# Giving the operations that empty a PSUM bank an earlier place in the scheduler's order

## The chip, the cores and the metric

The kernel runs on one NeuronCore of a Trainium2 chip. The metric is the device time of one execution in microseconds (us). Five engines matter: TensorE (PE in the profile) does matrix products into PSUM, which has eight banks of 128 partitions by 2 KB; VectorE (DVE) and ScalarE (ACT) work on PSUM and SBUF; GpSimd (POOL) and SyncE (SP) mainly issue DMA transfers here. Each engine runs its own list of instructions in the order in which the program was laid out, and waits on semaphores for the others.

## The reference

Eight sequences of 3008 positions with 256 channels go through a filter in the frequency domain, and every position of the result then goes through a two-layer network with a squared relu.

```python
X  = rfft(x, axis=1)                       # x: 8 x 3008 x 256
Yr = Xr @ w_r - Xi @ w_i + b_r
Yi = Xr @ w_i + Xi @ w_r + b_i
Y  = sign(Y) * max(abs(Y) - 0.01, 0)       # on Yr and Yi each
y  = irfft(Y, n=3008, axis=1).reshape(24064, 256)
out = (s * max(y @ w_in, 0)**2 + b) @ w_out    # d_ff 2048, back to 256
```

The inputs and the result are float32; the kernel's products take float16 operands and sum in float32.

## The kernel before, in words

**The transforms.** 3008 is 94 x 32, so both transforms are done as two smaller ones, as matrix products. For a batch there are four kinds of unit, each of which fills one PSUM bank and ends with an operation that empties it:
- `s1_units`: the first step (products `psf<-x,A_t`), emptied to `u` by `evac`, which goes out to DRAM as `ud` and comes back turned as `us`.
- `s23_units`: `fwd_unit` (`psf<-F_t,us`), emptied to `xf` by `evac`, and then the sum of two parts of `xf` on DVE (L672); `sum_unit` (`psf<-W_t,xf`), emptied to `s` by ACT (L686); `mix_unit` (`psf<-W_g,xf`), emptied by a DVE add into a buffer called `ring` (L699). `shrink` is the soft threshold on `ring` in three DVE operations (L714, L715, L716), after which SP moves the quarters of `ring` by DMA (L725). `inv_unit` (`psf<-ring,T_t`) is emptied to `v` by `evac`, and `v` goes through DRAM too.
- `s4_units`: the last step (`psf<-C_t,vs`), emptied to `yt` by `evac`. `yt` holds what the network takes as its tokens.

`evac` puts its copy on ACT (L187) or on DVE (L189), by two running estimates of how far each engine's work reaches (`load`, `work`, `act_first`).

**The network.** The token phase, which begins after the first batch's transforms, goes over tiles of up to 512 tokens. A tile has 16 slots (MC = 16 blocks of the hidden width). In slot `mc`, `first_mm` computes one block of `y @ w_in` into half of a double bank (`psh`); every second slot ACT applies the relu to `rt` (L871), and the square goes to `gt` on ACT (L881) or DVE (L884). The product with `w_out` of a tile runs one tile later, in slots beside the next tile's `first_mm`. It comes in two forms:
- `second_mms`: plain products into a `psa` bank, two halves to a bank, and one DVE operation that empties it to `ost` (L945).
- `seven_mms`, for some tiles: a block scheme with seven products in place of eight. It needs sums of blocks of `gt`, made in `s_op`: numbers 1, 2 and 3 on DVE (L980), number 4 as an accumulating DMA issued by POOL (L973). The products share banks in the groups (0, 1), (2), (3, 4) and (5, 6). `leave(group)` combines them: in group 0 an add into `zz` (L1012), an add into `ost` (L1012) and then `zz` plus a constant (L1030); in groups 1 to 3 more adds by L1012. The output goes to DRAM by SP's queue.

**Sharing the banks.** In the token phase the pools hold two double banks (`psh`), two single banks for the network's second product (`psa`) and two for the transforms (`psf`). A matmul that opens a bank anew waits until the operation that empties the bank's previous tile has ended.

**Sharing the time.** `plan` puts the units of the next batches' transforms into the slots of the current tiles, so that the program's text interleaves `first_mm`, the second product and transform units. All matmuls are issued by one helper and so carry one line, L175; the tiles' names tell them apart.

**What sets the order.** The framework numbers operations as the program issues them. When it lays out each engine's list, it goes by this number as priority among the operations that it deems ready by a model of its own. Inside `tc.high_priority(offset=200)` an operation gets a number 200 lower, so that it counts as if it had been issued 200 places earlier. An operation's place in one engine's list can also change what is deemed ready on another.

Of the kernel before, what the change touches and what calls it, by code (L numbers as in the profile page):

```python
# [1 line left out]

# [1 line left out]

# [7 lines left out]
ALU = mybir.AluOpType  # L12
AF = mybir.ActivationFunctionType

P = 128
# [81 lines left out]
def kernel(  # L97
# [79 lines left out]
    def work(engine, us):  # L177
        load[engine] = max(load[engine], pe["now"]) + us

    def act_first(ready, ta, td):  # L180
        return max(load["act"], ready) + ta <= max(load["dve"], ready) + td + lean[0]

    def evac(dst, src, cols):
        ta, td = over["act"] + cols / 1200.0, over["dve"] + cols / 960.0
        if act_first(pe["now"], ta, td):
            work("act", ta)
            return None, nc.scalar.copy(out=dst, in_=src)  # L187
        work("dve", td)
        return nc.vector.tensor_copy(out=dst, in_=src), None  # L189

    pools = {}

# [456 lines left out]
    def s23_units(b):  # L649

        vd = dpool.tile([NPAIR, P, D], F16, name="vd", tag="vd")
        if not ring:
            ring.append(bigpool.tile([P, 12, 2, D], F16, name="ring", tag="corr"))
        xf = {}
        zt = {}
        hold = {}

        def fwd_unit(i):

            bank = one_bank()  # L660
            ps = bank.rearrange("p (r c j k) -> p r c j k", r=2, c=DC, j=2)
            t = us[(b, i // 3)]
            for j in range(2):
                q = (2 * i + j) % 6
                for dc in range(DC):
                    matmul(
                        ps[:, :, dc, j, :], t[:, q, dc * P : (dc + 1) * P],
                        F_t[:, 2 * i + j, :], start=True, stop=True,
                    )
            xt = xfpool.tile([P, 3, DC, P], F16, name="xf", tag="xf")  # L670
            evac(xt[:, 1:3].rearrange("p r c k -> p (r c k)"), bank, 512)
            nc.vector.tensor_tensor(out=xt[:, 0], in0=xt[:, 1], in1=xt[:, 2], op=ALU.add)  # L672
            work("dve", 0.34)
            xf[i] = xt

        def sum_unit(h):

            ps = one_bank().rearrange("p (i e) -> p i e", i=2)
            for i in range(2):
                for dc in range(DC):  # L680
                    matmul(
                        ps[:, i, :], xf[2 * h + i][:, 0, dc], W_t[:, dc, 0],
                        start=(dc == 0), stop=(dc == DC - 1),
                    )
            s = mpool.tile([P, 2, D], F32, name="s", tag="m")
            nc.scalar.copy(out=s, in_=ps)  # L686
            work("act", 0.49)
            hold[h] = s

        def mix_unit(i):  # L690
            ps = one_bank().rearrange("p (r e) -> p r e", r=2)
            xt = xf.pop(i)
            for r in range(2):
                for dc in range(DC):
                    matmul(
                        ps[:, r, :], xt[:, 2 - r, dc], W_g[:, dc, r],
                        start=(dc == 0), stop=(dc == DC - 1),
                    )
            nc.vector.tensor_tensor(  # L699
                out=ring[0][:, i % 4], in0=ps,  # L700
                in1=hold[i // 2][:, i % 2].unsqueeze(1).to_broadcast([P, 2, D]), op=ALU.add,
            )
            work("dve", 0.67)
            if b == 1:
                shrink(i, 1)
            elif i % 2:
                shrink(i - 1, 2)

        def shrink(i, n):

            m0 = 4 + (i % 2 if n == 1 else 0)
            t, m = ring[0][:, i % 4 : i % 4 + n], ring[0][:, m0 : m0 + n]
            lo, hi = (v.unsqueeze(1).to_broadcast([P, n, 2, D]) for v in (low, high))
            nc.vector.tensor_tensor(out=m, in0=t, in1=lo, op=ALU.max)  # L714
            nc.vector.tensor_tensor(out=m, in0=m, in1=hi, op=ALU.min)  # L715
            nc.vector.tensor_tensor(out=t, in0=t, in1=m, op=ALU.subtract)  # L716
            work("dve", 0.21 + 0.8 * n)
            for k in range(i, i + n):
                z = ring[0][:, 6 + k % 6]
                for j in range(2):  # L720
                    for r in range(2):
                        o = z[64 * r : 64 * r + 64, j]
                        a = t[64 * j : 64 * j + 64, k - i, r]
                        if k < H - 2:
                            nc.sync.dma_start(out=o, in_=a)  # L725
                        else:
                            nc.vector.tensor_copy(out=o, in_=a)
                            work("dve", 0.13)
                zt[k] = z

        def inv_unit(i):
            ps = one_bank().rearrange("p (j e) -> p j e", j=2)
            z = zt.pop(i)
            for j in range(2):
                matmul(
                    ps[:, j, :], T_t[:, 2 * i + j, :], z[:, j, :], start=True, stop=True
                )
            if i % 2 == 0:
                hold["v"] = vpool.tile([P, 4, D], F16, name="v", tag="v")
            v = hold["v"]  # L740
            h = 2 * (i % 2)
            evac(v[:, h : h + 2, :], ps, 512)
            if i % 2 == 1:
                nc.sync.dma_start(
                    out=vd[2 * i - 2 : 2 * i + 2].rearrange("q p e -> p q e"), in_=v
                )
            if i == H - 1:
                hold["vv"] = vd.rearrange("q (k n) e -> (q k) (n e)", n=N2)
                take_half(0)
                if b == 1:  # L750
                    take_half(1)

        def take_half(h):
            t = vspool.tile([96, HW, D], F16, name="vs", tag="vs")
            nc.sync.dma_start(
                out=t.rearrange("k n e -> k (n e)"),
                in_=hold["vv"][:, h * HW * D : (h + 1) * HW * D],
            )
            vs[(b, h)] = t

        units = []

        def put(f, i, n):
            if 0 <= i < n:
                units.append(lambda: f(i))

        for h in range(H // 2 + 3):
            for i in range(2):
                put(fwd_unit, 2 * h + i, H)
                put(mix_unit, 2 * h - 2 + i, H)  # L770
                put(inv_unit, 2 * h - 6 + i, H)
            put(sum_unit, h, H // 2)
            if h == H // 2:
                units += [lambda: None] * 2
        return units, lambda: take_half(1)
# [75 lines left out]
    def first_mm(ti, mc):  # L851
# [16 lines left out]
        if mc % 2 == 0:  # L868
            return
        rt = rpool.tile([P, 2, 512], F32, name="rt", tag="rt")  # L870
        nc.scalar.activation(out=rt[:, :, 0:w], in_=ps[:, :, 0:w], func=AF.Relu)  # L871
        q, g = divmod(mc // 2, 4)
        if g == 0:
            gts[(ti, q)] = gpool.tile([P, 2, 2, 4, 2 * P], F16, name="gt", tag="gt")
# [47 lines left out]
    def second_mms(ti):  # L922
# [6 lines left out]
        def mm(sub, mc):  # L929

            alone = ti == len(tiles) - 1 and sub >= 2
            h = 0 if alone else sub % 2
            if h == 0 and mc == 0:
                hold["ps"] = sum_bank(ti).rearrange("p (h e) -> p h e", h=2)
            ps = hold["ps"]
            matmul(
                ps[0:size, h, :],
                lhs_of(ti, mc, sub),
                w_out_t[:, mc, :],
                start=(mc == 0), stop=(mc == MC - 1),  # L940
            )
            if mc == MC - 1 and (alone or h == 1 or sub == nsub - 1):
                k = h + 1
                ost = opool.tile([P, 2, D], F32, name="ost", tag="ost")
                nc.vector.scalar_tensor_tensor(  # L945
                    out=ost[0:size, 0:k], in0=ps[0:size, 0:k], scalar=s_bc[0:size],
                    in1=bias_bc[0:size].unsqueeze(1).to_broadcast([size, k, D]), op0=ALU.mult, op1=ALU.add,
                )
                work("dve", 0.13 + 0.27 * k)
                for i in range(k):  # L950
                    store(tl, sub - k + 1 + i, ost[:, i, :])
# [31 lines left out]
    def seven_mms(ti):  # L983
# [25 lines left out]
            )  # L1009

        def add(out, of, other):
            nc.vector.scalar_tensor_tensor(  # L1012
                out=out, in0=of, scalar=s_bc[0:size], in1=other, op0=ALU.mult, op1=ALU.add
            )
            work("dve", 0.4)

        def wide(t):
# [2 lines left out]
        def leave(group):  # L1020
# [6 lines left out]
            if group == 0:  # L1027
                add(z[:, 0], hold[0], wide(bias_bc))
                add(top[:, :, 0:P], hold[1], z[:, 0])
                nc.vector.tensor_tensor(out=z[:, 1], in0=z[:, 0], in1=wide(b_21), op=ALU.add)  # L1030
                work("dve", 0.34)
            elif group == 1:
                add(z[:, 0], hold[2], z[:, 0])
# [144 lines left out]
```

## Time and profile before

The times of three runs are 840.66, 837.92 and 838.69 us; the median is 838.69. The profile was taken of one execution.

| | |
|---|---|
| profiled execution: span, first to last instruction | 837.9 us |
| median of the runs, less this span | 0.8 us |
| PE busy (matmuls) | 822.6 us, 98%, 7662 matmuls |
| ACT busy | 723.0 us, 86%, 962 instructions |
| DVE busy | 706.9 us, 84%, 1104 instructions |
| POOL busy | 86.2 us, 10%, 114 instructions |
| granted clock of TensorE, mean | 0.996 |
| DMA moved | 107.17 MB, mean 128 GB/s |

The page gives each engine's busy time, the span in 40 slices, the DMA queues, the chain of work that ended last, groups of equal instructions with the idle time before them, and the DMA issues. A group is written as out<-in by the program's names, such as `psa<-T_s,s`. The trace behind it also answers questions of its own: what an engine waited for and how long (the list of waits), what ran in a stretch of time (the timeline, where a bracket at the end of a row is idle time of the engine before it and what ended it), and who waits for one line's instructions.

### The profile page before, as it was taken

The page shows a single profiled execution, that of the slowest core. Times are in us where ns is not written, and L with a number is a line of the kernel's source. Part 1 is how long each engine was busy: PE and PEld are TensorE (multiplying, and loading weights), DVE is VectorE, ACT ScalarE, POOL GpSimd, SP SyncE. Part 2 cuts the span into 40 slices and gives each one's busy share as a digit, 9 for nine tenths or more (in the row PEclk, how much of TensorE's full clock was granted, in tenths as well). Part 3 has the DMA queues.
Part 4 walks back from the last instruction along what each step waited for, and adds up shares of the span by engine and source line. Part 5 has one row for each costly group of instructions (what it writes and reads, how often), then busy time and mean ns, then how long its engine had stood idle before and what let it go on. Part 6 is the DMA issues. An engine that isn't in the chain of part 4 may idle for free.

```text
span 837.9 us, 19547 instructions
## 1 busy us (share of the span) xinstructions
PE 822.6 (98%) x7662; PEld 600.7 (72%) x7662; DVE 706.9 (84%) x1104; ACT 723.0 (86%) x962; POOL 86.2 (10%) x114
## 2 busy tenths in 40 slices
PE   8999999999999999999999999999999999999997
PEld 7857767777677767777677676767767777767765
DVE  5888989978898888988889888797889988889885
ACT  4998988998899989998889988989889988788882
POOL 4540001100011001100011000100001000001000
PEclk8999999999999999999999999999999999999999
DMA  8954578345873378444773368723565333513321
GB/s 196 180 153 103 124 189 203 63 94 133 198 185 65 94 184 208 114 104 128 195 185 69 88 147 208 175 63 105 127 178 138 67 100 93 137 45 77 72 65 60
DMA packets 116670, 107.17 MB, mean 128 GB/s; under 512 B 12774, under 2 KB 100842, under 8 KB 115234
## 3 DMA queue, kind: packets, MB, share of 16 engines
q1 hardware_dynamic: 102498, 80.55, 33.6%
q0 software_dynamic: 14080, 25.37, 19.1%
q8 instruction: 60, 0.98, 0.5%
q14 instruction: 32, 0.26, 0.1%
HBM read 53.52 MB, written 46.66 MB: 120 GB/s over the span
## 4 chain that ended last, share of the span: by engine, by line
PE 75%; DVE 12%; ACT 6%; DMA 3%; issue 3%; SPq 0%; POOL 0%; DVEq 0%; POOLq 0%
PE psh L175 31%; PE psa L175 28%; PE psf L175 16%; ACT rt L871 3%; DVE gt L884 2%; DVE gt L980 2%; ACT gt L881 1%; DVE ring L699 1%; PE psm L175 1%; DMA gt<-gt 1%; DVE ost L1012 1%; DMA ring<-ring 1%; DVE s L980 1%; DMA x<-in_x_dram 1%; DVE zz L1012 1%
## 5 line engine op out<-in xcount | busy, mean ns | idle before, releaser
L871 ACT ACTIVATE rt<-psh 128x1024 f32<-128x1024 f32 (+2 forms) x384 | 386.7, 1008 | 57.0 <-PE psh L175 55.1
L175 PEld LDWEIGHTS <-gt 128*128 128x128 f16 (+1 forms) x3696 | 304.8, 101 | 167.7 <-DMA gt<-gt 0.5
L175 PE MATMUL psh<-yt,w_in 128*128 128x512 f16 (+1 forms) x1344 | 397.1, 378 | 0.1
L884 DVE TENSOR_TENSOR gt<-rt 128x1024 f16<-128x1024 f32 (+2 forms) x239 | 286.2, 1202 | 78.6 <-ACT rt L871 77.6
L175 PE MATMUL psa<-w_out_t,gt 128*128 128x256 f16 (+3 forms) x2448 | 310.9, 253 | 0.3 <-DMA gt<-gt 0.3
L175 PEld LDWEIGHTS <-w_in 128*128 128x128 f16 x1536 | 136.5, 98 | 24.4 <-issue 1.7
L881 ACT ACTIVATE gt<-rt 128x1024 f16<-128x1024 f32 (+2 forms) x145 | 150.8, 1040 | 3.4
L175 PE MATMUL psa<-T_s,gt 128*128 128x128 f16 (+1 forms) x944 | 79.4, 219 | 0.0
L973 POOL DMA_DIRECT2D gt<-gt x42 | 38.0, 905 | 316.2 <-PE psh L175 66.3
L187 ACT CAST u<-psf 96x512 f16<-96x512 f32 x96 | 55.6, 581 | 9.3 <-PE psf L175 8.6
L699 DVE TENSOR_TENSOR ring<-psf,s 128x512 f16<-128x512 f32 x84 | 57.7, 686 | 3.5 <-PE psf L175 2.5
L187 ACT CAST v<-psf 128x512 f16<-128x512 f32 x79 | 45.8, 583 | 13.6 <-PE psf L175 13.5
L234 POOL DMA_DIRECT2D x<-in_x_dram x36 | 19.2, 539 | 325.1 <-PE psf L175 324.0
L175 PE MATMUL psh<-tail,w_in 128*128 128x512 f16 (+1 forms) x192 | 52.1, 353 | 0.0
L175 PEld LDWEIGHTS <-xf 128*128 128x128 f16 x504 | 46.6, 98 | 6.6 <-DVE xf L672 1.5
L175 PE MATMUL psf<-W_g,xf 128*128 128x256 f16 x336 | 50.4, 272 | 0.0
L187 ACT CAST yt<-psf 128x470 f16<-128x470 f32 (+2 forms) x84 | 43.3, 534 | 3.4 <-PE psf L175 2.2
L1012 DVE SCALAR_TENSOR_TENSOR ost<-psa,s_bc,zz 128x256 f32<-128x256 f32 (+1 forms) x80 | 35.9, 480 | 9.8 <-PE psa L175 8.2
L187 ACT CAST xf<-psf 128x512 f16<-128x512 f32 x64 | 37.4, 585 | 4.2 <-PE psf L175 3.9
L945 DVE SCALAR_TENSOR_TENSOR ost<-psa,s_bc,bias_bc 128x512 f32<-128x512 f32 (+2 forms) x51 | 37.1, 727 | 3.8 <-PE psa L175 1.4
L175 PE MATMUL psf<-x,A_t 94*96 94x512 f16 x102 | 39.0, 382 | 1.4 <-ACT yt L187 0.3
L175 PE MATMUL psf<-C_t,vs 96*128 96x94 f16 (+1 forms) x484 | 37.9, 205 | 0.0
(118 smaller groups left out, 802.6 us busy)
## 6 DMA issues: line engine op xcount, KB each, us to landing
out_dram<-ost SPq DMA_DIRECT2D x152, 128.0 KB
ud<-u SPq DMA_DIRECT2D x56, 192.0 KB
us<-ud SPq DMA_DIRECT2D x28, 384.0 KB
vd<-v SPq DMA_DIRECT2D x42, 256.0 KB
vs<-vd SPq DMA_DIRECT2D x14, 768.0 KB
x<-in_x_dram POOLq DMA_DIRECT2D x28, 376.0 KB, 6.0
gt<-gt POOLq DMA_DIRECT2D x38, 256.0 KB, 4.4
ring<-ring SPq DMA_DIRECT2D x280, 32.0 KB
```

The lines of the kernel that those rows point to most:

```text
L175: return nc.tensor.matmul(out, lhs, rhs, **how)
L187: return None, nc.scalar.copy(out=dst, in_=src)
L234: nc.gpsimd.dma_start(out=t[0:N1, i * w : (i + 1) * w], in_=xv[:, c * XCH * D + i * w : c * XCH * D + (i + 1) * w],)
L699: nc.vector.tensor_tensor(out=ring[0][:, i % 4], in0=ps, in1=hold[i // 2][:, i % 2].unsqueeze(1).to_broadcast([P, 2, D]), op=ALU.add,)
L871: nc.scalar.activation(out=rt[:, :, 0:w], in_=ps[:, :, 0:w], func=AF.Relu)
L881: nc.scalar.activation(out=gt, in_=rr, func=AF.Square)
L884: last_square[0] = nc.vector.tensor_tensor(out=gt, in0=rr, in1=rr, op=ALU.mult)
L945: nc.vector.scalar_tensor_tensor(out=ost[0:size, 0:k], in0=ps[0:size, 0:k], scalar=s_bc[0:size], in1=bias_bc[0:size].unsqueeze(1).to_broad ...
L973: nc.gpsimd.dma_start(out=a12, in_=a11, accum_op=ALU.add)
L980: nc.vector.tensor_tensor(out=out, in0=a, in1=b, op=op)
L1012: nc.vector.scalar_tensor_tensor(out=out, in0=of, scalar=s_bc[0:size], in1=other, op0=ALU.mult, op1=ALU.add)
```

## The change

A helper `urgent()` gives `tc.high_priority(offset=200)` in the token phase (`pe["on"]`) and does nothing before it. It is put round the operations that read a PSUM bank and so free it, in `evac` (both engines), `sum_unit`, `mix_unit`, `first_mm`, `second_mms` and the `add` of `seven_mms`, and round one that reads none: `zz` plus a constant in `leave(0)`.

```diff
+    def urgent():
+
+        return tc.high_priority(offset=200) if pe["on"] else nullcontext()
+
     def evac(dst, src, cols):
         ta, td = over["act"] + cols / 1200.0, over["dve"] + cols / 960.0
-        if act_first(pe["now"], ta, td):
-            work("act", ta)
-            return None, nc.scalar.copy(out=dst, in_=src)
-        work("dve", td)
-        return nc.vector.tensor_copy(out=dst, in_=src), None
+        with urgent():
+            if act_first(pe["now"], ta, td):
+                work("act", ta)
+                return None, nc.scalar.copy(out=dst, in_=src)
+            work("dve", td)
+            return nc.vector.tensor_copy(out=dst, in_=src), None
...
             s = mpool.tile([P, 2, D], F32, name="s", tag="m")
-            nc.scalar.copy(out=s, in_=ps)
+            with urgent():
+                nc.scalar.copy(out=s, in_=ps)
...
-            nc.vector.tensor_tensor(
-                out=ring[0][:, i % 4], in0=ps,
-                in1=hold[i // 2][:, i % 2].unsqueeze(1).to_broadcast([P, 2, D]), op=ALU.add,
-            )
+            with urgent():
+                nc.vector.tensor_tensor(
+                    out=ring[0][:, i % 4], in0=ps,
+                    in1=hold[i // 2][:, i % 2].unsqueeze(1).to_broadcast([P, 2, D]), op=ALU.add,
+                )
...
         rt = rpool.tile([P, 2, 512], F32, name="rt", tag="rt")
-        nc.scalar.activation(out=rt[:, :, 0:w], in_=ps[:, :, 0:w], func=AF.Relu)
+        with urgent():
+            nc.scalar.activation(out=rt[:, :, 0:w], in_=ps[:, :, 0:w], func=AF.Relu)
...
                 ost = opool.tile([P, 2, D], F32, name="ost", tag="ost")
-                nc.vector.scalar_tensor_tensor(
-                    out=ost[0:size, 0:k], in0=ps[0:size, 0:k], scalar=s_bc[0:size],
+                with urgent():
+                    nc.vector.scalar_tensor_tensor(
+                        out=ost[0:size, 0:k], in0=ps[0:size, 0:k], scalar=s_bc[0:size],
...
         def add(out, of, other):
-            nc.vector.scalar_tensor_tensor(
-                out=out, in0=of, scalar=s_bc[0:size], in1=other, op0=ALU.mult, op1=ALU.add
-            )
+            with urgent():
+                nc.vector.scalar_tensor_tensor(
+                    out=out, in0=of, scalar=s_bc[0:size], in1=other, op0=ALU.mult, op1=ALU.add
+                )
             work("dve", 0.4)
...
-                nc.vector.tensor_tensor(out=z[:, 1], in0=z[:, 0], in1=wide(b_21), op=ALU.add)
+                with urgent():
+                    nc.vector.tensor_tensor(
+                        out=z[:, 1], in0=z[:, 0], in1=wide(b_21), op=ALU.add
+                    )
```

More of the change, by code (lines that the diff above doesn't have):

```diff
@@ L1 @@
-from contextlib import ExitStack
+from contextlib import ExitStack, nullcontext
 import numpy as np
@@ L944, in mm @@
                 ost = opool.tile([P, 2, D], F32, name="ost", tag="ost")
-                nc.vector.scalar_tensor_tensor(
-                    out=ost[0:size, 0:k], in0=ps[0:size, 0:k], scalar=s_bc[0:size],
-                    in1=bias_bc[0:size].unsqueeze(1).to_broadcast([size, k, D]), op0=ALU.mult, op1=ALU.add,
-                )
+                with urgent():
+                    nc.vector.scalar_tensor_tensor(
+                        out=ost[0:size, 0:k], in0=ps[0:size, 0:k], scalar=s_bc[0:size],
+                        in1=bias_bc[0:size].unsqueeze(1).to_broadcast([size, k, D]),
+                        op0=ALU.mult, op1=ALU.add,
+                    )
                 work("dve", 0.13 + 0.27 * k)
@@ L1011, in add @@
         def add(out, of, other):
-            nc.vector.scalar_tensor_tensor(
-                out=out, in0=of, scalar=s_bc[0:size], in1=other, op0=ALU.mult, op1=ALU.add
-            )
+            with urgent():
+                nc.vector.scalar_tensor_tensor(
+                    out=out, in0=of, scalar=s_bc[0:size], in1=other, op0=ALU.mult, op1=ALU.add
+                )
             work("dve", 0.4)
@@ L1029, in leave @@
                 add(top[:, :, 0:P], hold[1], z[:, 0])
-                nc.vector.tensor_tensor(out=z[:, 1], in0=z[:, 0], in1=wide(b_21), op=ALU.add)
+                with urgent():
+                    nc.vector.tensor_tensor(
+                        out=z[:, 1], in0=z[:, 0], in1=wide(b_21), op=ALU.add
+                    )
                 work("dve", 0.34)
```

## The prediction

> **What bounds the kernel now.** I read the page's busy shares and slices first, then the groups, the list of TensorE's waits, the timeline round the longest of them, the rows of one line and last the chain.
>
> The page's busy shares, and three rows of its slices:
>
> ```profile
> PE 822.6 (98%) x7662; PEld 600.7 (72%) x7662; DVE 706.9 (84%) x1104; ACT 723.0 (86%) x962; POOL 86.2 (10%) x114
> ...
> PE   8999999999999999999999999999999999999997
> ...
> PEclk8999999999999999999999999999999999999999
> ```
>
> PE is the bound from the second slice on, at a granted clock of 0.996 over the span. The change adds and removes no matmul, so it can win only idle time of PE, and lose only by making more of it. What there is, from the list of PE's waits:
>
> ```profile
> engine line waited for: us in total, times, longest us
> PE psa L175 <- DVE ost L1012: 4.5, 8, 0.9
> PE psm L175 <- DMA x<-in_x_dram: 2.1, 2, 1.5
> PE psa L175 <- DVE ones L241: 1.0, 1, 1.0
> PE psa L175 <- DVE z L509: 0.4, 2, 0.2
> PE psf L175 <- ACT yt L187: 0.3, 1, 0.3
> PE psa L175 <- DMA gt<-gt: 0.3, 1, 0.3
> ```
>
> The second to fourth lie in the first batch, which the change leaves as it is. The first is a bank emptied late: `seven_mms` puts two products in each psa bank, two banks exist, and the third product waits for `leave(0)` to drain the first bank. Going by starts of matmuls that lie further apart than their columns take (0.056 us per 128 columns in an undisturbed row), five of these waits are long: 0.73 at 170.3, 0.91 at 360.6, 0.90 at 462.9, 1.07 at 562.2 and 0.91 at 664.6; with a scatter of smaller ones all gaps after 40 us come to some 13 to 16 us. One of the five in the timeline:
>
> ```profile
> 460.48 0.69 DVE L980 TENSOR_TENSOR gt<-gt 128x1024 f16<-128x1024 f16 x1
> ...
> 461.08 0.69 DVE L715 TENSOR_TENSOR ring<-ring,high 128x1024 f16<-128x1024 f16 x1
> ...
> 461.69 0.69 DVE L980 TENSOR_TENSOR gt<-gt,s 128x1024 f16<-128x1024 f16 x1
> ...
> 462.29 0.69 DVE L716 TENSOR_TENSOR ring<-ring 128x1024 f16<-128x1024 f16 x1
> ...
> 462.89 0.48 DVE L1012 SCALAR_TENSOR_TENSOR zz<-psa,s_bc,bias_bc 128x256 f32<-128x256 f32 x1
> ...
> 463.28 0.29 DVE L672 TENSOR_TENSOR xf<-xf 128x256 f16<-128x256 f16 x1
> 463.48 0.49 DVE L1012 SCALAR_TENSOR_TENSOR ost<-psa,s_bc,zz 128x256 f32<-128x256 f32 x1
> ...
> 464.02 0.61 PE L175 MATMUL psa<-T_s,s 128*128 128x128 f16 x8 [0.75 <-DVE ost L1012]
> ```
>
> The bank's last matmul was done at 459.99, but four SBUF operations of DVE stand before the first add. From start to start they take 0.60 each, an L1012 add 0.39.
>
> **The change, part by part.** Both kernels' instruction orders, laid side by side, show that the instructions are the same and that some places of each engine's order are exchanged. Six parts matter; times are those of before's trace.
>
> 1. The five long waits. On DVE, `zz` now stands right behind the first L980, and L715 between the two adds: `zz` at 461.08, L715 461.47, `ost` 462.07 to 462.56, so the bank is free 1.4 us earlier. That alone would end the wait. But PE's order moves too: its first product from `s` used to stand behind four W_g, two psh, two T_t and one more psh matmul, and now stands ahead of them, right behind the T_s matmuls that end at 461.8. PE arrives 1.3 us earlier and waits from 461.80 to 462.61, 0.81 in place of 0.91: a gain of 0.10. By the same rows 0.10 at 360, 562 and 664. At 170 `zz` moves further and the wait goes from 0.73 to 0.42: 0.31. Sum 4 x 0.10 + 0.31 = **0.7 gained** of 4.5. The matmuls that are now behind the wait start up to 0.8 later; of what they feed, the relu (L871) and square are wanted a tile later (some 16 us) and DVE comes to L699 at 463.8, when W_g has ended at 463.3.
> The Trainium skill, PSUM — Partial Sum Buffer, section Summary: rules for kernel authors, says to empty PSUM promptly. By that rule the whole 4.5 would come back; by the rows it is 0.7, because the earlier drain draws the waiting matmul with it. No run here yet tells them apart.
>
> 2. What is pushed back there. The second L980 (`s_op` 2 of quarter 1) goes behind `zz`, `ost`, zz+b, L716, the next `zz` and L699: 2.1 us later at 170 and 2.7 at the other four. PE reads its result first at 465.78 and it will be ready at 465.1: covered by 0.6. POOL's accumulating DMA (L973) waits for it. From the rows of that line:
>
> ```profile
> who waited for it (us, times):
> ...
>   PE psa L175: 0.3, 1
> ...
> DMA to landing us min/median/max: 3.3/4.5/8.8
> ```
>
> Landed before against wanted by PE: 365.25 and 368.97, 467.28 and 471.26, 567.84 and 570.73, 668.73 and 672.93. So 2.9 to 4.2 us of cover against 2.7, nothing lost if landing takes as long as before (0.2 us is left at 562). At 170 it landed at 178.10 and PE wanted it at 178.57, 0.47 of cover against 2.1: between 0 (if it lands in the 4.5 of the median, as it was slowed by traffic that may be over) and 1.6 (if in 7.39 as before). I take the middle: **0.8 lost**.
>
> 3. The same DMA at 237, 428 and 630, where only `zz` (0.39) moves ahead of L980: the bank is free 0.12 earlier at 237 and 630, **0.24 gained**. At 428 it is the chain's longest DMA,
>
> ```profile
> 428.45 8.84 DMA gt<-gt
> ```
>
> landed at 437.29, and PE already loses 0.44 to it at 437.3. 0.39 later costs between 0 and 0.39: **0.3 lost**, by the nearest row, its own. At 237 and 630 1.5 us of cover remain.
>
> 4. Three waits for a psf bank at 81.2 (0.42), 87.0 (0.18 with its neighbours) and 295.3 (0.18): an L699 or an `xf` copy moves ahead of an SBUF operation of 0.60 to 1.2. The first halves, the others go: 0.2 + 0.2 + 0.2, **0.55 gained**.
>
> 5. At some eleven tile ends the third add of `leave(3)` passes a square (L884), which comes 0.2 to 0.39 later. Its readers on PE have 0.19 to 0.75 of slack; at 764 and 777 it falls short, 0.1 + 0.2 = **0.3 lost**. At the same places DVE fills a hole of 0.1 to 0.25 in which it waited for the relu, so the `xf` sums come some 0.14 earlier and the waits at 250, 340, 443 and 644 shrink: **0.5 gained**. These sizes are single gaps of the trace and the least sure.
>
> 6. Costed at nothing: L699 passing a square in some 20 places (the square has over 1.3 us of slack), u and xf copies passing a square on ACT, and in SP's queue the u stores passing eight ring DMAs at 203, 393, 495 and 595 (ring 0.6 later, read 5.6 to 8 us after its issue), out stores passing them at 555 (1.6 later). POOL's order stays. If that cover were gone, each would cost its delay, 0.4 to 1.6.
>
> Sum: 0.7 + 0.24 + 0.55 + 0.5 gained, 0.8 + 0.3 + 0.3 lost: net 0.6 gained. The profiled span is 837.9; by the sum 837.3. The median of the runs is 838.69, 0.8 above the span, so 838.1.
>
> **The rivals.**
>
> *Faster.* PE's order in the trace's conditions need not cost what I count: if DVE runs ahead of the rows above (it was behind by a backlog of SBUF operations that the new order spreads out), `ost` is done when PE arrives. Then the 4.5 goes whole: 4.5 + 0.24 + 0.55 + 0.5 - 1.4 = 4.4, **834.3**. For it: DVE has idle time (84%). Against it: `zz` can't start before DVE ends the L980 in front of it at 461.08, and the two adds and L715 between them make 1.5 us. It decides if L715 did not stand between and PE's order had stayed.
>
> *Slower.* The accumulating DMA becomes PE's wait. Issued 2.1 to 2.7 later at five places, with a landing of 7.4 us as at 170 (rows of 6.2 to 8.8 are frequent while other transfers run) PE would wait 1.6 at 170, (360.70 + 2.7 + 7.4) - 368.97 = 1.8 at 360, 1.8 at 462, 2.6 at 562 and 1.8 at 664: 9.6, less the 2.0 of gains, **846**; with two of the five late, 841. It decides when landing takes over 5.6 us (562) or 6.7 (462). For it: 428. Against it: the four landed in 4.1 to 4.6. Whether POOL's issue (0.86 here) is held by DVE's work is the same question, and no row shows it.
> The Trainium skill, DMA: Bandwidth & Descriptors, section Issuing engines are not separate DMA queues, says that transfers of all issuers interleave on the same sixteen engines; that speaks for landing times that depend on the moment of issue, and this trace agrees with 3.3 to 8.8 us for equal transfers.
>
> *No effect at all* would need an unchanged order, which the listing excludes; a change that only exchanges waits is the forecast.
>
> **How the numbers follow.** 0.3% is 2.5 us, about what a measurement of this kernel can tell from no change (its three runs lie 2.7 apart). The forecast, 838.1, has 0.62, with its own range of 836.6 to 840; the faster rival, in part or whole, 0.15; the slower one, in part or whole, 0.23, of which one in five stays inside 0.3%. So faster 0.16, same 0.64, slower 0.20. The range reaches down to half of the faster rival's gain and up to two late DMAs: 835.6 to 841.6.
>
> **What would show it.** Right: the first line of PE's waits falls from 4.5 to about 3.8 with PE's `s` products a microsecond earlier than before; L973's issue at the five places 2 to 3 us later in its tile, with PE's waits for gt<-gt under 1.5 in all. Wrong: that first line under 1 (faster rival), or waits for gt<-gt of over 3 us (slower rival), or a new releaser, such as L871 or L980, in the list.

## The result and the profile after

The changed kernel takes 837.15 us (median of 18 runs, 835.59 to 840.58), the kernel before, beside it, 839.33 us (18 runs, 837.92 to 842.11). The ratio is 0.9971 with a 95% interval of 0.9959 to 0.9982: faster by 2.4 us, between 1.5 and 3.4. That is 0.29%, at the very edge of the 0.3% that the prediction called "same".

The profiled execution after has a span of 835.7 us and a time of 837.46, so 1.8 us lie around the span; before's span of 837.9 thus belongs to an execution of about 839.6, not to the 838.69 of the three runs then known. The page's busy shares after:

```profile
PE 820.7 (98%) x7662; PEld 598.5 (72%) x7662; DVE 703.9 (84%) x1104; ACT 723.0 (87%) x962; POOL 86.3 (10%) x114
```

The instructions are as many as before, and PE is still the bound. The list of PE's waits after (the lines are those of the changed kernel: L1023 was L1012):

```profile
engine line waited for: us in total, times, longest us
PE psa L175 <- DVE ost L1023: 3.5, 7, 0.8
PE psm L175 <- DMA x<-in_x_dram: 2.9, 6, 0.7
PE psa L175 <- DVE ones L246: 1.0, 1, 1.0
PE psf L175 <- DMA ring<-ring: 0.9, 1, 0.9
```

The first line fell from 4.5 to 3.5. A wait for a ring transfer is new, and before's 0.3 for gt<-gt is gone. The site that the prediction showed, in the timeline after (start, duration, engine and operation, and in brackets PE's idle time before it):

```profile
459.09 0.68 DVE L990 TENSOR_TENSOR gt<-gt 128x1024 f16<-128x1024 f16 x1
...
459.69 0.48 DVE L1023 SCALAR_TENSOR_TENSOR zz<-psa,s_bc,bias_bc 128x256 f32<-128x256 f32 x1
...
460.07 0.50 PE L175 MATMUL psa<-T_s,gt 128*128 128x128 f16 x6
460.08 0.68 DVE L722 TENSOR_TENSOR ring<-ring,high 128x1024 f16<-128x1024 f16 x1
460.68 0.48 DVE L1023 SCALAR_TENSOR_TENSOR ost<-psa,s_bc,zz 128x256 f32<-128x256 f32 x1
...
461.22 0.23 PE L175 MATMUL psa<-T_s,s 128*128 128x128 f16 x1 [0.65 <-DVE ost L1023]
461.23 0.37 PEld L175 LDWEIGHTS <-xf 128*128 128x128 f16 x4
461.28 0.49 PE L175 MATMUL psf<-W_g,xf 128*128 128x256 f16 x3
```

DVE now empties the bank 1.4 us earlier after its last product (2.6 us in place of 4.0). But one product `psa<-T_s,s` now stands right behind the T_s,gt products and ahead of W_g, and PE waits there: by starts of matmuls 0.81 us, where it was 0.90.

Two things in these traces are scatter. The 501st matmul, with the same instructions ahead of it, starts anywhere between 43.7 and 47.5 us in the thirteen traces taken (44.86 before, 44.05 after). The two latest, e6_seven_shift at 46.9 and e4_old_shift at 47.5, are those whose granted clock between 15 and 20 us was 0.66 and 0.50, where it was 1.00 in all the others. And three kinds of wait for transfers come and go between executions of one kernel: a T_t product for `ring` near 110 us, a C_t product for `vs` near 320, and products for `gt<-gt`. So the traces are compared below from the 501st matmul to the last, with the gaps at those waits taken off (us against the first trace of before):

| kernel | ratio of times, 95% | 501st to last matmul | gaps at those transfers | rest, against before |
|---|---|---|---|---|
| before; again | 1 | 0; +0.4 | 0.7; 1.0 | 0; +0.1 |
| changed; again | 0.9971 (0.9959 to 0.9982) | -1.1; -2.4 | 1.7; 0.4 | -2.1; -2.0 |
| e1_seven | 0.9978 (0.9968 to 0.9988) | -1.6 | 0.3 | -1.2 |
| e2_rest | 0.9995 (0.9982 to 1.0008) | -0.45 | 0.9 | -0.6 |
| e3_shift | 0.9940 (0.9924 to 0.9956) | -3.0 | 2.3 | -4.6 |
| e4_old_shift | 0.9993 (0.9980 to 1.0005) | -0.9 | 0.3 | -0.5 |
| e5_sop | 0.9935 (0.9913 to 0.9957) | -3.1 | 3.0 | -5.4 |
| e6_seven_shift | 0.9945 (0.9926 to 0.9965) | -2.6 | 2.7 | -4.5 |
| e8_leave0 | one run | -0.6 | 0.8 | -0.7 |
| e9_leave123 | one run | +0.4 | 1.4 | -0.3 |

The last column repeats within 0.1 us for both kernels of which there are two traces. It is no measure of time for an edit that makes those transfers later, so the column to its left stands beside it.

### The profile page after: what moved, and what is told of

Read it like the earlier page. It is cut to its first block, busy times and chain, and to the rows that moved or that the text cites. A ratio compares the mean times of both kernels' runs of the same rounds, so it can differ in the third digit from the quotient of the medians.

```text
span 835.7 us, 19552 instructions
## 1 busy us (share of the span) xinstructions
PE 820.7 (98%) x7662; PEld 598.5 (72%) x7662; DVE 703.9 (84%) x1104; ACT 723.0 (87%) x962; POOL 86.3 (10%) x114
## 4 chain that ended last, share of the span: by engine, by line
PE 78%; DVE 9%; ACT 5%; DMA 5%; issue 2%; POOL 0%; SPq 0%; DVEq 0%; POOLq 0%
PE psh L175 32%; PE psa L175 28%; PE psf L175 17%; ACT rt L879 2%; DVE gt L892 2%; DMA vd<-v 1%; DMA ring<-ring 1%; DMA x<-in_x_dram 1%; DVE ring L706 1%; DVE gt L990 1%; PE psm L175 1%; DVE ost L1023 1%; DMA vs<-vd 1%; ACT gt L889 1%; DVE s L990 1%
## 5 line engine op out<-in xcount | busy, mean ns | idle before, releaser
L706 DVE TENSOR_TENSOR ring<-psf,s 128x512 f16<-128x512 f32 x84 | 57.4, 684 | 4.1 <-PE psf L175 3.1
L1023 DVE SCALAR_TENSOR_TENSOR ost<-psa,s_bc,zz 128x256 f32<-128x256 f32 (+1 forms) x80 | 34.7, 477 | 7.9 <-PE psa L175 6.4
```

The source lines that it names most:

```text
L706: nc.vector.tensor_tensor(out=ring[0][:, i % 4], in0=ps, in1=hold[i // 2][:, i % 2].unsqueeze(1).to_broadcast([P, 2, D]), op=ALU.add,)
L1023: nc.vector.scalar_tensor_tensor(out=out, in0=of, scalar=s_bc[0:size], in1=other, op0=ALU.mult, op1=ALU.add)
```

## The experiments

### Which operations carry the gain: e1_seven and e2_rest

The edit of e1_seven: every `urgent()` except those in `seven_mms` is undone, at five places of which one is shown. That of e2_rest is the opposite.

```diff
-            with urgent():
+            with nullcontext():
                 nc.scalar.copy(out=s, in_=ps)
```

> The higher priority is left on the adds of seven_mms (L1023 and zz plus a constant) alone. Theory: these carry the gain. In the changed kernel's trace the waits that they touch shrink: 0.50 at 170, 0.13 at 237, 0.43 in all at the four long ones, 0.6 round 428 and 436, 0.19 at 630, 0.5 at the xf sums: 2.4 us, so a time about 2.4 us below the kernel before (ratio 0.997). The rival: the copies and adds that empty psf and psh carry it; then this kernel is within 0.5 us of the kernel before.

> The higher priority is left on everything except the adds of seven_mms. Theory: worth nothing or less; the psf waits at 81, 108 and 295 go (0.7 us), but the T_t product that waited 1.0 us for a ring transfer at 110.7 in the changed kernel waits here too, if that wait comes from the order: between 0.7 us faster and 0.5 slower than the kernel before. The rival, that these operations carry the gain, expects 2 us faster.

Measured: 837.29 us, 1.8 us faster than before (interval 1.0 to 2.7), and 839.02, no difference (0.7 us slower to 1.5 faster). In the traces the rest is -1.2 and -0.6, together -1.8, against -2.0 and -2.1 for the whole change. The adds of `seven_mms` carry most of it. The rival, that the copies out of psf and psh do, falls. e2_rest has no ring wait near 110 although its order there is that of the changed kernel on all engines, so the expectation's condition, that this wait comes from the order, is not met.

### Which of the adds: e8_leave0 and e9_leave123

The edit: from e1_seven, the priority is kept on the three operations of `leave(0)` only, or on the other groups only.

```diff
-        def add(out, of, other):
-            with urgent():
+        def add(out, of, other, first=False):
+            with urgent() if first else nullcontext():
```

> The higher priority on the three operations of leave(0) alone. Theory (steps 1 and 3): the waits for L1023 go from 0.73, 0.91, 0.90, 1.07, 0.91 to 0.23, 0.81, 0.81, 0.97, 0.81, and 0.13, 0.19 and 0.19 go at 237, 428 and 630: from the start of the token phase the trace is 1.1 to 1.5 us shorter than that of the kernel before; the xf waits at 340 and 644 (0.18, 0.24) stay. A rival, that the last group's adds carry the gain: under 0.5.

> The higher priority on the adds of leave(1), leave(2) and leave(3) alone. Theory (step 5): the xf waits at 250, 340, 443 and 644 shrink, 0.5 us, less a later square at 764 and 777 (0 to 0.3): 0.2 to 0.6 us shorter from the start of the token phase, the waits for L1023 as before (4.5 us). The rival expects over 1 us.

Measured, in one run each: the rests are -0.7 and -0.3, which make up most of e1_seven's -1.2. In e8_leave0 the long waits are 0.42, 0.81, 0.81, 0.98 and 0.81, and PE's order is the one of e1_seven; the xf waits at 340 and 643 stay (0.18, 0.21). It also has the wait that the prediction priced at 0.8: 0.57 us for `gt<-gt` at 177. With it the whole is 0.6, below the 1.1 to 1.5 expected. So moving the operations of `leave(0)` on DVE is enough to move PE's products. In e9_leave123 PE's order is that of before, the long waits at 361, 463, 562 and 665 are as before (0.91, 0.90, 1.06, 0.90), the xf waits at 340, 442 and 644 are gone, and a 1.1 us wait for `vs` near 321 covers it all.

### Where the rest of the gain went: e3_shift and e4_old_shift

The edit, on the changed kernel (e3_shift) and on the kernel before (e4_old_shift), is one line: the first product of number 3 goes from the end of one slot to the head of the next, behind that slot's psh products.

```diff
-            slots[at // 7].append(lambda w=what: mm(*w))
+            slots[at // 7 + (what == (3, 0, 0))].append(lambda w=what: mm(*w))
```

> The changed kernel, with the first product of number 3 of seven_mms issued at the head of the next slot, behind that slot's two psh products (and a transform unit where there is one), which is 0.4 to 0.9 us of PE work. Theory (step 1 of the prediction: the earlier drain is eaten by PE's earlier arrival): the nine waits for L1023 that the changed kernel still has (0.39, 0.23, 0.18, 0.81, 0.81, 0.44, 0.93, 0.81, 0.44: 5.0 us) nearly all go; 4 to 5 us below the changed kernel, some 832.5, ratio to the kernel before 0.992 to 0.993. The rival, that DVE's backlog is the limit and the wait comes back at the next bank (groups 1 and 2): less than 2 us below the changed kernel.

> The kernel before, with that same product moved to the head of the next slot and no priority changed. Theory: at the five long waits PE's order had this place or a later one already and DVE's order is the old one, so they stay (4.5 us); only the six short ones can go (0.39, 0.31, 0.19, 0.43, 0.19, 0.44): at most 1.9 us below the kernel before. The rival, that the place of the product alone is what matters, expects 5 us or more below.

Measured: e3_shift 834.54 us (6 runs, 834.03 to 835.18), 5.0 us faster than before (3.7 to 6.4) and 2.6 us below the changed kernel's median, where 4 to 5 had been expected; e4_old_shift 838.74, no clear difference (at most 1.7 us faster). In PE's waits of e4_old_shift (whose lines are numbered as in the changed kernel) the five long ones are left, 0.74, 0.90, 0.90, 1.07 and 0.91 by starts:

```profile
PE psa L175 <- DVE ost L1023: 3.7, 5, 0.9
```

In e3_shift no wait for L1023 over 0.08 us is left, and the same site reads:

```profile
459.28 0.50 PE L175 MATMUL psa<-T_s,gt 128*128 128x128 f16 x6
...
459.62 0.60 PE L175 MATMUL psf<-W_g,xf 128*128 128x256 f16 x4
459.89 0.48 DVE L1023 SCALAR_TENSOR_TENSOR ost<-psa,s_bc,zz 128x256 f32<-128x256 f32 x1
...
460.49 0.61 PE L175 MATMUL psa<-T_s,s 128*128 128x128 f16 x8
```

PE does the W_g and psh products while DVE empties the bank, and has no idle time of its own before T_s,s. Neither order alone does this: DVE's order with PE's early product gives 2.4 us, PE's late product with DVE's old order at most 1.7, both together 5.0. The theory of step 1 stands in its mechanism; its size does not, since 5.0 us of waits went and the time fell by 2.6. The rival holds in part: DVE's backlog does bring a wait back, though not the whole. What takes their place in e3_shift's trace: 0.27 to 0.32 at four places for the L990 that step 2 follows (a product `psa<-T_s,gt` at 361, 463, 562 and 663), 0.3 for `gt<-gt` at 177 and 0.2 at 535, and 0.2 to 0.35 for a psf bank at the C_t product next in line (136, 529, 725).

### Can the L990 be had early too: e5_sop and e6_seven_shift

The edit of e5_sop on e3_shift; e6_seven_shift is e3_shift with the priorities of e1_seven.

```diff
-        nc.vector.tensor_tensor(out=out, in0=a, in1=b, op=op)
+        early = tc.high_priority(offset=190) if n == 2 and q == 1 else nullcontext()
+        with early:
+            nc.vector.tensor_tensor(out=out, in0=a, in1=b, op=op)
```

> The changed kernel with the product moved as in e3_shift, and the second L980 of the pair (a11 minus s1 of quarter 1, the one that the change pushed behind four or five other operations) at a priority 190 places higher, so that it stands between the two adds of leave(0) in place of L715. Theory: in e3_shift PE waited 0.27, 0.27, 0.32 and 0.29 for it at the four late places and 0.28 for the accumulating DMA at 177; these 1.4 us go and the bank comes free as early as in e3_shift: 1 to 1.5 us below e3_shift, 833 to 833.5. The rival: the thresholds on ring and their transfers, now 1 to 2 us later, become waits of the T_t products, or the bank comes later: no gain on e3_shift, or a loss of up to 2 us.

> The product moved as in e3_shift, the higher priority on the adds of seven_mms alone. Theory: the other operations' priority is worth about 0.5 us by e2_rest, less what the ring transfer at 110 cost in e3_shift (0.7 to 1.0); so within 0.7 us of e3_shift on either side, with no ring wait at 110. The rival, that the pair of edits needs the other operations' priority too: 1.5 us or more above e3_shift.

Measured: 834.73 (833.08 to 835.95) and 834.61 (833.90 to 838.86), neither to be told from e3_shift. In e5_sop the four L990 waits are gone, and other waits have taken part of their place: a psf bank for A_t at 373 and 474 waits 0.48 for `v` on DVE (0.21 in e3_shift), and ring waits near 110 are 2.0 us in this trace. The rest is 0.8 us below e3_shift's; the times don't show it, and the 1 to 1.5 us expected did not come. In e6_seven_shift, too, the four waits are gone without the L990 being moved: there L706 has no priority and doesn't pass it. It was expected to have no ring wait near 110 and has one of 1.3 us, in an order there which is that of before on all engines: this wait doesn't need the change.

### The same kernels once more: c_after and c_before

> The changed kernel once more, for a second trace. If the 1.0 us wait of a T_t product for a ring transfer at 110.7 belongs to the order, it is there again with 0.8 to 1.2 us; if it belongs to how the transfers happened to fall, it is under 0.3 or elsewhere. The waits for L1023 should repeat within 0.05 each.

> The kernel before once more, for a second trace. The waits for L1012 should repeat within 0.05 each (0.73, 0.91, 0.90, 1.07, 0.91); the start of the token phase, which lay between 40.6 and 44.4 us in the traces so far with the same instructions in front of it, should differ by a microsecond or more again, which says that this part of the time is scatter and not the change.

Measured: the changed kernel 836.19 us with no ring wait near 110 (the largest gap there is 0.15), and the L1023 waits 0.23, 0.83, 0.81, 0.93 and 0.81, within 0.02 of the first trace. The kernel before 839.11, with 0.73, 0.90, 0.90, 1.07 and 0.90; the 501st matmul started 1.0 us earlier than in its first trace. So the 1.0 us ring wait in the first trace of the changed kernel, and 0.8 of the 2.2 us between the two first spans, are not the change.

### What the slower rival would take: e7_dma2

The edit, on the changed kernel; the other engines' orders stay.

```diff
+    idle = cpool.tile([P, 32], F16, name="idle", tag="idle")
...
+            if q == 0:
+                nc.gpsimd.dma_start(out=a12, in_=a11, accum_op=ALU.add)
+                return
+            nc.gpsimd.tensor_copy(out=idle[0:1, 0:1], in_=a11[0:1, 0, 0:1])
+            for _ in range(16):
+                last = nc.gpsimd.memset(idle, 0.0)
+            with tc.issue_after(last.ins):
+                nc.gpsimd.dma_start(out=a12, in_=a11, accum_op=ALU.add)
```

> The changed kernel, where POOL does about 2 us of idle work (a one-element copy that waits for the operand, then sixteen small memsets of a scratch tile) ahead of each accumulating DMA of quarter 1; the order on the other engines is the same. It asks how much cover those DMAs have. In the second trace of the changed kernel the DMAs landed this far ahead of PE's use: 1.08, 0.16, 0.88, 1.80, 0.61, 1.78, 1.43, 1.12, 1.45, 1.44, 1.87, 1.79, 0.13 and 1.84 us at the tight places. If a transfer takes as long when issued later (the slower rival's rule), PE loses what is short of 2 us: 10 to 11 us, time about 848. If the long transfers shorten by what they are issued later, as at 170 (7.4 us before, 5.3 to 5.4 after), only the places with a landing of 3.3 to 4.5 us lose: 2 to 4 us, about 840. If the DMA doesn't bound anything: under 1 us.

Measured: 854.02 us, ratio 1.0161 (1.0126 to 1.0196). The delay came out at 3.0 to 3.1 us and not 2: a memset took 0.125 and the next followed 0.06 later. PE's waits:

```profile
PE psa L175 <- DMA gt<-gt: 14.7, 11, 2.0
PE psa L175 <- DVE ost L1031: 3.5, 7, 0.8
```

With 3.0 us in the place of 2, the fourteen tight places lack 10.6 + 14 x 1.0 = 25 us if each transfer takes as long as before; the gaps at gt<-gt in the trace sum to 16.5 over eleven. Places are named here by the issue in the second trace of the changed kernel. Where the transfer had taken 3.6 or 3.7 us it took 3.4, and PE lost nearly all that was short (1.1 of 1.2 at 361 and 463, 1.7 of 1.9 at 563). Three long ones shortened by a third and more: 5.3 to 3.6 us (at 171), 7.3 to 4.4 (at 426) and 6.5 to 3.7 (at 628), and the last two cost nothing. Two other long ones hardly did (6.6 to 6.5 at 135, 6.8 to 6.4 at 236). So neither of the two rules that the expectation weighed holds alone. The rival's mechanism is real; the change stopped short of it.

## Why the prediction was right

The time lies in the range, and the direction and the main steps hold. The net gain was forecast at 0.6 us and is 2.4 (1.5 to 3.4), four times as much. That it still counts as "same", by 0.29% against 0.3%, is luck. That the steps named the right waits and the reason why the large ones stay is not.

**Step 1, right.** 0.10 at each of four places and 0.31 at 170 were forecast; about 0.10, 0.09, 0.14, 0.10 and 0.50 were found, 0.92 in place of 0.7, and the first line of PE's waits fell to 3.5 for the 3.8 forecast. At 170 PE's wait fell to 0.23, not 0.42; with `leave(0)` alone it is 0.42, and with the later groups alone 0.55, so the other groups' adds give the remaining 0.2. The explanation, that PE's earlier arrival eats the earlier drain, is shown by e8_leave0, which moves the same products on PE, and by e3_shift and e4_old_shift. The Trainium skill, PSUM — Partial Sum Buffer, section Summary: rules for kernel authors, asks for prompt emptying. By itself that brought 2.4 us here, and the 5.0 came only when the matmul that needs the bank was held back too.

**Step 2, the term that failed.** The 0.8 us lost to the late accumulating DMA at 170 did not come: 0 in both traces of the changed kernel. Issued 1.9 us later, the transfer took 5.4 us in place of 7.4 and landed at 178.00. That is the lower end of the step's own bounds, 0, with nothing to spare: PE came to its product 0.05 us after the landing in the first trace of the changed kernel and 0.16 in the second, and 0.05 is also what passes between landing and product where PE does wait for it. Over the traces this transfer takes 7.4 to 7.9 us where it has its old place in the order (before twice, e2_rest, e4_old_shift, e9_leave123), and 5.3 to 6.8 at a later one (changed kernel twice, e1_seven, e3_shift, e5_sop, e6_seven_shift, e8_leave0). e8_leave0, e3_shift, e5_sop and e6_seven_shift do lose 0.2 to 0.6 there. At the other four places the issue came 2.7 later and nothing was lost, both as forecast, with 1.1 to 1.9 us left (not 0.2 at 562, where the transfer took 3.5 in place of 4.6). The Trainium skill, DMA: Bandwidth & Descriptors, section Issuing engines are not separate DMA queues, has all issuers' transfers interleave on the same engines. Equal transfers of 3.2 to 8.8 us in these traces agree with it, but no run here varied the other traffic.

**Step 3, half wrong.** 0.13 at 237 and 0.19 at 630 were found for the 0.24 forecast. At 428 a loss of 0.3 was forecast; the bank wait of 0.19 went, and the 0.44 for `gt<-gt` is absent after. But it is absent in the second trace of before as well, so it is not the change's.

**Step 4, right in size.** 81.2 fell from 0.42 to 0.15, 295 went, the 0.18 near 87 moved to 88 and stayed: 0.45 for 0.55. A fourth wait for a psf bank, 0.23 at 108, went too; no step of the prediction names it.

**Step 5, right where it was least sure.** The xf waits give 0.10 at 250, 0.18 at 340 and 0.24 at 644, 0.5 in all, and 0.09 or 0.23 more at 443, by the two traces of before. The later square costs 0.15 at 763 and nothing at 777, for the 0.3 forecast.

**Step 6, as far as seen.** No new wait for the moved u stores or ring transfers appears in the second trace after.

So the gains were priced at 2.0 and are 2.4 (0.9, 0.5, 0.45 and 0.5), 2.7 to 2.8 with the waits at 108 and 443, and the losses at 1.4 and are 0.15. Small gaps elsewhere that grew take some 0.5 back, which leaves the 2.0 and 2.1 of the table. The error is mainly one of size and lies in the losses of steps 2, 3 and 5: each was taken near the middle or the far end of its bounds, and of 1.4 us only 0.15 came. A second error is in the sum's last line: the time around the span is 1.8 us, not the 0.8 from comparing one span with the median of other runs, so that the forecast of a 837.3 span meant 839.1. The two errors pull opposite ways, and that the forecast of 838.1 lies within 1 us of the 837.15 owes something to this. And two figures of the slower rival do not come out of its own rows: the landing that decides is 570.73 - 563.24 - 2.7 = 4.8 us at 562 and 471.26 - 463.00 - 2.7 = 5.6 at 462, not 5.6 and 6.7, so that it stood closer than it says.

**The rivals.** The faster one (PE's waits for L1012 go whole) did not happen. e3_shift makes half of its condition, PE's later product, and there those waits go, although the ring operation (L722) still stands between the two adds. The slower one did not happen either: what it costs at each place is shown by e7_dma2, 1.1 to 2.2 us at eleven places for a delay of 3.0.

## What to carry to other kernels

When an operation is moved forward in a scheduler's order, look at what the scheduler then does with the instruction that waited for it: a bank that comes free 1.4 us earlier gave 0.1 us, since the waiting matmul was drawn 1.3 us forward, and moving that one matmul back behind ready work was worth as much again (2.6 us) as the whole change. An in-order engine gains when the release comes early and the use comes late; check both orders. Before a difference of a quarter of a per cent is read from two traces, take each trace twice: here the start-up differed by up to 3.8 us and the three transfer waits by up to 2.7, for a change of 2.4.

## What the runs showed of the hardware that was not expected

- An accumulating DMA of 256 KB, issued 1.9 us later, landed at the same time (178.1 and 178.0 us), so 2 of its 7.4 us hung on the moment of issue; issued another 3.1 later in e7_dma2, it took 3.6. Of the other long ones two shortened by some 40% with that delay and two hardly at all. What held them wasn't tried.
- Waits of a T_t product for a 32 KB ring transfer near 110 us were between nothing and 2.0 us in thirteen traces, before the first tile that the order of `seven_mms` touches; what makes them was not found.
- The 501st matmul started between 43.7 and 47.5 us in the same order, and the latest starts go with the granted clock: eleven traces have 43.7 to 44.9, the two with a clock of 0.66 and 0.50 between 15 and 20 us have 46.9 and 47.5. In those 5 us PE was busy for 4.8 us in e4_old_shift, at 0.50, with 32 matmuls, and for 4.8 us in the second trace of before, at 1.00, with 54. The first trace of before had 0.54 between 10 and 15 us and is the latest of the eleven. The times agree: of 49 runs of the kernel before, the 12 with a mean clock of 0.997 or less have a median of 840.6 us, the other 37 one of 839.1. What lowered the clock was not found.
